# Spectral mixing and a two-layer MLP in split fp32: weight split earlier, high parts first, half of layer 0's casts on ScalarE

## The chip, the cores and the metric

The kernel runs on one core of one Trainium2 chip. What is compared is the device time of one execution in microseconds, the median of several runs. Within an execution, a trace of the hardware profiler tells when each instruction of each engine ran: TensorE (PE; its weight loads are PEld), VectorE (DVE), ScalarE (ACT), GpSimd (POOL), and SyncE (SP), which issues most of the transfers.

## What is computed

```python
X = np.fft.rfft(x, axis=1)                    # x: 2 x 3008 x 256
Yr = Xr @ w_r - Xi @ w_i + b_r
Yi = Xr @ w_i + Xi @ w_r + b_i
Y  = sign(Y) * max(|Y| - 0.01, 0)             # real and imaginary part, each
x  = np.fft.irfft(Y, n=3008, axis=1).reshape(6016, 256)
h  = x @ w_in1;  g = max(h, 0) + alpha * min(h, 0);        x = g @ w_out1     # 256 -> 2048 -> 256
h  = x @ w_in2;  g = h if h >= 1, 0 if h <= -1, else (h + 1)**2 / 4;  return g @ w_out2
```

The weights of the MLP layers are float64; everything is wanted with an accuracy beyond that of one reduced product, so each fp32 operand of the large products is split into a rounded high part and the rest, the low part, and a product is made of three: low x high, high x low, high x high.

## The kernel before, in words

**Stages.** The transform over 3008 = 47 x 64 points is done in two steps. First, `f1(g)` for 16 groups of inputs (8 for each of the 2 sequences): products with a 96 x 96 constant, copied out by ScalarE and VectorE in turn, stored to a scratch `a_dr` in DRAM (`store_a`) and loaded again in another order (`load_a`, in six parts for each sequence; `A_PARTS` gives first column and number of columns, and part (6, 6) holds the columns of items 3 to 5). Then 24 items (b, i) run through `f2` (second transform step), `mix` (product with the complex weights, soft threshold) and `i1` (first step of the inverse transform); item j's `mix` runs behind item j + 2's `f2`, apart from the first, where `f2` of items 2 and 3 follows `mix` of item 0. `p3` is the last step of the inverse transform. The two MLP layers follow.

**Mixing.** The weights `wm32[k]` are loaded by SyncE (lines 279 and 281), and `split` (lines 86 to 92) makes the high part as a cast on ScalarE (line 89) or VectorE (line 91) and the low part as a subtraction on VectorE (line 92). For the weights this is done behind the last `f1` (lines 302 to 304). An item's own parts are made in `f2`: high parts on ScalarE (lines 319, 320), low part on VectorE (line 321), its negated piece on ScalarE (line 322). `mix` has 24 products an item, in groups low x high, high x low, high x high (lines 335 to 337), the one with the item's low part first.

**MLP.** Each layer goes through 12 chunks of tokens (512 columns, chunks 5 and 11 have 448). For each chunk there are 16 steps f. `first(l, c, f)` makes six products into a PSUM bank (`psh`), then the nonlinearity: in layer 0 two relus on ScalarE into `ta` and `tb` (lines 447, 448) and a combination on VectorE (line 450), in layer 1 a relu on ScalarE and two operations on VectorE. The result is split into `gh` and `gl`. `ta` and `tb` have two buffers each, `gh` and `gl` four. `second(l, c, f)` makes six products of `gh` and `gl` into two banks that sum up over the 16 steps (`pso`); at f = 15 ScalarE copies the two banks out (line 479). The order is written out by hand in the last loop (lines 534 to 563): at each position `first` of one step, then side work, then `second` of the step three positions back (`DEPTH`). Each engine works through its own instructions in program order.

**Late and early casts.** `late_split` (line 421) names the steps whose cast is done late: all of layer 1, chunks 0, 1 and 11 of layer 0. There `split_late` inside the *next* step's `first` (line 449) issues the cast on ScalarE, behind that step's relus, and the subtraction on VectorE, ahead of that step's combination. For the other chunks of layer 0, 2 to 10, cast and subtraction follow the combination at once, both on VectorE (line 452).

**Side work in layer 0.** The weights of layer 1 are converted from float64 by a generator, `conversions`; each `next(conv)` (line 553) issues one piece, in chunks 2 to 10 on steps f = 0, 4, 8, 12. A piece in two parts: every second `next` issues a cast and two conversions on ScalarE (lines 175, 146, 147), two operations on VectorE (164, 148) and a multiplication and a clamp on GpSimd (165, 180); the one after that an operation on VectorE (159) and a subtraction and an addition on GpSimd (169, 170), which GpSimd can begin as soon as the first are done. On f = 8 `prep` splits the next chunk's input (128 x 1024: a cast on ScalarE, a subtraction on VectorE).

Of the kernel before, what the change touches and what calls it, by code (L numbers as in the profile page):

```python
# [9 lines left out]
F32R = mybir.dt.float32r  # L10
# [6 lines left out]
B, S, D = 2, 3008, 256  # L17
# [4 lines left out]
NF = DFF // 128  # L22
# [53 lines left out]
def spectral_mlp_kernel(ctx: ExitStack, tc: tile.TileContext, x, w_r, w_i, bias, c_f1, c_f2,  # L76
                        c_i1, c_i2, w_in1, w_out1, alpha, w_in2, w_out2, out):
    nc = tc.nc
    V, A, G, T = nc.vector, nc.scalar, nc.gpsimd, nc.tensor
# [6 lines left out]
    def split(src, hi, lo, hi_engine):  # L86

        if hi_engine is A:
            A.activation(hi, src, AF.Copy)  # L89
        else:  # L90
            V.tensor_copy(hi, src)  # L91
        V.tensor_tensor(lo, src, hi.bitcast(F32), op=ALU.subtract)  # L92
# [10 lines left out]
    def block(tag, shape, dtype, name):  # L103
        return base.tile(shape, dtype, tag=tag, name=name)
# [77 lines left out]
    def conversions(l, fs, clamp, low_engine):  # L182

        n = len(fs)
        for f in fs[:2]:
            load_w(l, f)
            yield
        for k in range(n + 1):
            if k >= 1:
                convert_w(l, fs[k - 1], 2, clamp, low_engine)  # L190
            if k < n:
                convert_w(l, fs[k], 0, clamp, low_engine)
            yield
            if k >= 1:
                convert_w(l, fs[k - 1], 3, clamp, low_engine)
            if k < n:
                convert_w(l, fs[k], 1, clamp, low_engine)
            if k + 2 < n:
                load_w(l, fs[k + 2])
            yield  # L200
# [23 lines left out]
    A_PARTS = ((0, 2), (2, 2), (4, 2), (6, 6), (12, 6), (18, 6))  # L224

    def load_a(b, parts):
        if a_sb[b] is None:
            a_sb[b] = block(f"a{b}", [128, NK, D], F32, f"a_{b}")
        for k, n in parts:
            h, k0 = divmod(k, NK // 2)  # L230
            src = a_dr[b][h].rearrange("t (q k) f -> (t q) k f", q=4)
            nc.sync.dma_start(a_sb[b][:, k:k + n, :], src[:, k0:k0 + n, :])
# [13 lines left out]
    def f1(g):  # L246
        b, j = divmod(g, 8)
        if g < 10:
            ae = block(f"w{8 + g}" if g < 5 else f"m{1 + g}" if g < 8 else f"w{g - 8}", [96, 4, D], F32, f"ae{g}")
        else:  # L250
            if g == 10:
                late.append(block("a1", [96, 6, 4, D], F32, "ae_late"))
            ae = late[0][:, g - 10]
        aes[g] = ae
        for i in range(2):
            ps = psum.tile([96, 2, D], F32, tag="h" if i else "o", name=f"ps1_{b}_{j}_{i}")
            for u in range(2):
                T.matmul(ps[:, u, :], c47, xs[g][:, 2 * i + u, :], start=True, stop=True)  # L258
            if i == 0:
                A.activation(ae[:, 0:2, :], ps, AF.Copy)  # L260
            else:
                V.tensor_copy(ae[:, 2:4, :], ps)
# [6 lines left out]
    wm32 = [rot.tile([128, 2, D], F32, tag="tb", name=f"wm32_{k}") for k in range(2)]  # L269
# [7 lines left out]
        if g == 3:  # L277
            load_mn(0, m_t, c_f2, 0)
    nc.sync.dma_start(wm32[0], w_r.rearrange("(c p) e -> p c e", p=128))
    load_a(0, A_PARTS[:1])  # L280
    nc.sync.dma_start(wm32[1], w_i.rearrange("(c p) e -> p c e", p=128))
    load_a(0, A_PARTS[1:2])
    nc.sync.dma_start(b_t[:, 0, :], bias)
    load_mn(0, m_t, c_f2, 1)
    load_a(0, A_PARTS[2:4])
# [8 lines left out]
    load_mn(2, m_t, c_f2)  # L294
    conv = conversions(0, list(range(NF)), V, V)
    next(conv)
    for g in range(8, 16):
        f1(g)
        store_a(g, 0)
    wm = [block(f"c{k}", [128, 2, 2, D], F32R, f"wm{k}") for k in range(2)]  # L300

    for k in range(2):
        hi, lo = (wm[k][:, z].rearrange("p c (h q) -> p c q h", h=2) for z in range(2))
        split(wm32[k].rearrange("p c (q h) -> p c q h", h=2), hi, lo, A)


    items = [(b, i) for b in range(B) for i in range(NK // 2)]
# [17 lines left out]
    def mix(b, i):  # L325
        xh, xl = xt.pop((b, i))
        ps = psum.tile([128, 2, D], F32, tag="o", name=f"psm{b}_{i}")
        for k in range(2):
            o = ps[:, k, :].rearrange("p (q h) -> p q h", h=2)
            for c in range(2):  # L330
                j = 2 * k + c
                for r, off in ((0, 64), (1, 0)):
                    last = c == 1 and r == 1
                    wh, wl = (wm[r][:, z, c, :].rearrange("p (h q) -> p q h", h=2) for z in range(2))
                    T.matmul(o, xl[:, j, off:off + 128], wh, start=c == r == 0, stop=False)  # L335
                    T.matmul(o, xh[:, j, off:off + 128], wl, start=False, stop=False)  # L336
                    T.matmul(o, xh[:, j, off:off + 128], wh, start=False, stop=last)  # L337
        cl_ = rot.tile([128, 2, D], F32, tag="ta", name=f"clip{b}_{i}")
        t = rot.tile([128, 2, D], F32, tag="tb", name=f"t{b}_{i}")
        y32 = rot.tile([128, 2, D], F32, tag="gh", bufs=4, name=f"y32_{b}_{i}")  # L340
        V.tensor_tensor(t, ps, b_t.to_broadcast([128, 2, D]), op=ALU.add)
        V.tensor_scalar(cl_, t, LAM, -LAM, op0=ALU.min, op1=ALU.max)
        V.tensor_tensor(y32, t, cl_, op=ALU.subtract)
        y_32[b, i] = y32
# [21 lines left out]
    NC = len(chunks)  # L366
# [52 lines left out]


    def late_split(step):
        return step[0] == 1 or step[1] < 2 or step[1] == NC - 1

    def split_late(step):
        if step is not None and late_split(step):
            split_g(step, A)
# [56 lines left out]
    n = len(items)  # L483
# [3 lines left out]
    for j in range(n):  # L487
# [23 lines left out]
        if j >= P3_AT:  # L511
            g = j - P3_AT
# [21 lines left out]
    for i in range(len(seq) + DEPTH):  # L534
        if i < len(seq):
            l, c, f = seq[i]
            if (l, c, f) == (0, 2, 0):
                for _ in conv:
                    pass
                conv = conversions(1, list(range(15)), G, G)  # L540
            if (l, c, f) == (0, NC - 1, 4):
                for _ in conv:
                    pass
                conv = conversions(1, [15], V, V)
            if i >= 1:
                first(l, c, f, seq[i - 1])
            if i == 2:
                prep(0, 1)
            if 8 <= i < 24 and i % 2 == 0:
                p3(4 + i // 2, 0)  # L550
                p3(4 + i // 2, 1)
            if 3 <= i < 2 * NF and i % 3 != 0 or l == 0 and c >= 2 and f % (2 if c == NC - 1 else 4) == 0:
                next(conv, None)
            if (l, c, f) == (0, 0, NF - 1):
                prep(0, 2)
            elif f == NF // 2 and (l, c) not in ((0, 0), (0, 1)):
                nxt = (l, c + 1) if c + 1 < NC else (l + 1, 0)
                if nxt[0] < 2:
                    prep(*nxt)
        elif i == len(seq):  # L560
            split_late(seq[-1])
        if i >= DEPTH:
            second(*seq[i - DEPTH])
# [30 lines left out]
```

## Time and profile before

| | us |
|---|---|
| median of 3 runs (lowest, highest) | 1153.89 (1153.33, 1154.28) |
| the profiled execution, device time | 1152.67 |
| span of its trace, first to last instruction | 1150.9 |
| TensorE busy | 1143.0 (99%) |
| VectorE busy | 905.9 (79%) |
| ScalarE busy | 633.4 (55%) |
| GpSimd busy | 85.1 (7%) |

The granted TensorE clock is 0.999 of full speed over the span. TensorE's busy time is modelled from pipelined products; how close it is to its limit is read from the distance of one product's start to the next. The chain that ended last is 93% TensorE and 4% VectorE.

### The profile page before, as it was taken

The numbers are of one execution on the slowest core, as the hardware profiler recorded it, in microseconds if no ns is written. First come the engines' busy times: TensorE is split into PE (matmuls) and PEld (weight loads), VectorE is DVE, ScalarE is ACT, GpSimd is POOL, SyncE is SP. The second block draws the span as 40 slices with busy tenths as digits, with TensorE's granted clock in tenths as the row PEclk, the third lists the DMA queues.
The fourth block names the chain that finished last, engine by engine and source line by source line (L and its number), as shares of the span: only waits on it lengthen the run. The fifth ranks groups of instructions, "written<-read, shape, count | busy, mean of one in ns | idle before, by whom it ended". The sixth has DMA issues, their size and how long they took to land.

```text
span 1150.9 us, 15833 instructions
## 1 busy us (share of the span) xinstructions
PE 1143.0 (99%) x5862; PEld 1026.1 (89%) x5862; DVE 905.9 (79%) x1409; ACT 633.4 (55%) x1131; POOL 85.1 (7%) x64
## 2 busy tenths in 40 slices
PE   9999999999999999999999999999999999999998
PEld 7899988988888988888889988888889988888898
DVE  3679977568899999999986687777777777777776
ACT  3455777675655655556555654545445454544544
POOL 0000000000132322312210000000000000000000
PEclk9999999999999999999999999999999999999999
DMA  9996561100010100100000000000000000000000
GB/s 290 311 306 206 187 189 41 56 1 1 19 37 20 37 19 19 37 19 19 1 1 19 1 1 19 1 19 19 19 1 19 17 1 19 19 19 1 20 19 16
DMA packets 37900, 59.30 MB, mean 52 GB/s; under 512 B 3328, under 2 KB 25280, under 8 KB 37824
## 3 DMA queue, kind: packets, MB, share of 16 engines
q1 hardware_dynamic: 37568, 58.15, 15.7%
q8 instruction: 46, 0.75, 0.3%
q14 instruction: 30, 0.25, 0.1%
q10 hardware_dynamic: 256, 0.15, 0.0%
HBM read 39.55 MB, written 18.74 MB: 51 GB/s over the span
## 4 chain that ended last, share of the span: by engine, by line
PE 93%; DVE 4%; ACT 1%; DMA 1%; issue 1%; SPq 0%; DVEq 0%; ACTq 0%
PE pso L96 13%; PE pso L97 13%; PE pso L95 13%; PE psh L95 13%; PE psh L97 13%; PE psh L96 13%; PE ps L258 2%; PE ps L416 2%; PE psm L335 2%; PE psm L337 2%; PE psm L336 2%; PE psi L350 2%; PE psf L314 2%; DVE gl L92 1%; DVE ta L450 1%; DVE gh L91 1%
## 5 line engine op out<-in xcount | busy, mean ns | idle before, releaser
L92 DVE TENSOR_TENSOR gl<-ta,gh 128x512 fp32r<-128x512 f32 (+1 forms) x384 | 273.5, 712 | 53.1 <-ACT gh L89 48.0
L96 PE MATMUL pso<-gl,w 128*128 128x512 f32 (+1 forms) x768 | 288.3, 375 | 1.2 <-DVE gl L92 1.1
L95 PE MATMUL pso<-gh,w 128*128 128x512 f32 (+1 forms) x768 | 288.4, 376 | 0.0
L95 PE MATMUL psh<-mxh,w 128*128 128x512 f32 (+1 forms) x768 | 288.2, 375 | 0.1
L96 PE MATMUL psh<-mxl,w 128*128 128x512 f32 (+1 forms) x768 | 287.8, 375 | 0.0
L97 PE MATMUL psh<-mxh,w 128*128 128x512 f32 (+1 forms) x768 | 287.7, 375 | 0.0
L97 PE MATMUL pso<-gh,w 128*128 128x512 f32 (+1 forms) x768 | 287.7, 375 | 0.0
L455 ACT ACTIVATE ta<-psh 128x512 f32<-128x512 f32 (+1 forms) x192 | 113.4, 591 | 242.9 <-PE psh L97 214.4
L447 ACT ACTIVATE ta<-psh 128x512 f32<-128x512 f32 (+1 forms) x192 | 113.3, 590 | 197.8 <-DVE gl L92 97.3
L456 DVE SCALAR_TENSOR_TENSOR tb<-ta 128x512 f32<-128x512 f32 (+1 forms) x192 | 130.8, 681 | 115.8 <-ACT ta L455 115.0
L450 DVE SCALAR_TENSOR_TENSOR ta<-ta,nalpha,tb 128x512 f32<-128x512 f32 (+1 forms) x192 | 157.8, 822 | 12.7 <-ACT tb L448 12.3
L96 PEld LDWEIGHTS pso<-gl,w 128*128 128x128 f32 x768 | 145.1, 189 | 20.3 <-DVE gl L92 3.1
L95 PEld LDWEIGHTS psh<-mxh,w 128*128 128x128 f32 x768 | 145.2, 189 | 17.8 <-ACT tb L448 0.5
L96 PEld LDWEIGHTS psh<-mxl,w 128*128 128x128 f32 x768 | 145.2, 189 | 17.6 <-DVE mxl L92 0.3
L97 PEld LDWEIGHTS psh<-mxh,w 128*128 128x128 f32 x768 | 145.2, 189 | 17.2
L95 PEld LDWEIGHTS pso<-gh,w 128*128 128x128 f32 x768 | 145.2, 189 | 17.1 <-DVE gh L91 0.2
L97 PEld LDWEIGHTS pso<-gh,w 128*128 128x128 f32 x768 | 145.2, 189 | 17.1
L89 ACT ACTIVATE gh<-ta 128x512 fp32r<-128x512 f32 (+1 forms) x240 | 147.4, 614 | 1.3 <-DVE ta L458 1.3
L458 DVE TENSOR_TENSOR ta<-psh,tb 128x512 f32<-128x512 f32 (+1 forms) x192 | 129.1, 672 | 0.0
L448 ACT ACTIVATE tb<-psh 128x512 f32<-128x512 f32 (+1 forms) x192 | 112.2, 584 | 0.0
L91 DVE CAST gh<-ta 128x512 fp32r<-128x512 f32 (+1 forms) x144 | 71.6, 497 | 15.2 <-DVE ta L450 0.5
L335 PE MATMUL psm<-wm,fl 128*128 128x256 f32 x192 | 54.9, 286 | 1.5 <-DVE fl L321 1.5
(56 smaller groups left out, 935.0 us busy)
## 6 DMA issues: line engine op xcount, KB each, us to landing
u<-in_w_in SPq DMA_DIRECT2D x32, 256.0 KB, 2.9
u<-in_w_out SPq DMA_DIRECT2D x32, 256.0 KB, 3.3
v_dr<-ve SPq DMA_DIRECT2D x12, 512.0 KB, 3.5
v<-v_dr SPq DMA_DIRECT2D x16, 384.0 KB, 5.6
x<-in_x SPq DMA_DIRECT2D x15, 384.0 KB, 7.6
out<-yt SPq DMA_DIRECT2D x20, 256.0 KB, 2.0
a<-a_dr SPq DMA_DIRECT2D x6, 768.0 KB, 7.3
a_dr<-ae SPq DMA_DIRECT2D x20, 192.0 KB, 6.7
```

The source lines that it names most:

```text
L89: A.activation(hi, src, AF.Copy)
L91: V.tensor_copy(hi, src)
L92: V.tensor_tensor(lo, src, hi.bitcast(F32), op=ALU.subtract)
L95: T.matmul(ps, wl, xh, start=start, stop=False)
L96: T.matmul(ps, wh, xl, start=False, stop=False)
L97: T.matmul(ps, wh, xh, start=False, stop=stop)
L447: A.activation(ta, ps, AF.Relu, scale=-1.0)
L448: A.activation(tb, ps, AF.Relu)
L450: V.scalar_tensor_tensor(ta, ta, nalpha[:, f:f + 1], tb, op0=ALU.mult, op1=ALU.add)
L455: A.activation(ta, ps, AF.Relu, bias=0.5, scale=0.5)
L456: V.scalar_tensor_tensor(tb, ta, 1.0, ta, op0=ALU.min, op1=ALU.mult)
L458: V.tensor_tensor(ta, ps, tb, op=ALU.max)
```

## The change

The weights of the mixing are split inside the loop of the last eight `f1`, the first behind group 13, the second behind group 14. The second weight is loaded ahead of the first part of the spectrum instead of behind it. `mix` takes, for each of the two weights, first the item's high part with the weight's low part, then high with high, then the item's low part. In layer 0, chunks 2 to 10, every second step (f odd) is cast late on ScalarE. The pieces of the conversion come on steps f = 2, 6, 10, 14 of these chunks.

```diff
     nc.sync.dma_start(wm32[0], w_r.rearrange("(c p) e -> p c e", p=128))
-    load_a(0, A_PARTS[:1])
     nc.sync.dma_start(wm32[1], w_i.rearrange("(c p) e -> p c e", p=128))
-    load_a(0, A_PARTS[1:2])
+    load_a(0, A_PARTS[:2])
...
+    wm = [block(f"c{k}", [128, 2, 2, D], F32R, f"wm{k}") for k in range(2)]
     for g in range(8, 16):
         f1(g)
         store_a(g, 0)
-    wm = [block(f"c{k}", [128, 2, 2, D], F32R, f"wm{k}") for k in range(2)]
-
-    for k in range(2):
-        hi, lo = (wm[k][:, z].rearrange("p c (h q) -> p c q h", h=2) for z in range(2))
-        split(wm32[k].rearrange("p c (q h) -> p c q h", h=2), hi, lo, A)
+        if g in (13, 14):
+
+            hi, lo = (wm[g - 13][:, z].rearrange("p c (h q) -> p c q h", h=2) for z in range(2))
+            split(wm32[g - 13].rearrange("p c (q h) -> p c q h", h=2), hi, lo, A)
...
-            for c in range(2):
-                j = 2 * k + c
-                for r, off in ((0, 64), (1, 0)):
-                    last = c == 1 and r == 1
-                    wh, wl = (wm[r][:, z, c, :].rearrange("p (h q) -> p q h", h=2) for z in range(2))
-                    T.matmul(o, xl[:, j, off:off + 128], wh, start=c == r == 0, stop=False)
-                    T.matmul(o, xh[:, j, off:off + 128], wl, start=False, stop=False)
-                    T.matmul(o, xh[:, j, off:off + 128], wh, start=False, stop=last)
+
+            for n, (r, x, z) in enumerate(((0, xh, 1), (0, xh, 0), (0, xl, 0), (1, xh, 1), (1, xh, 0), (1, xl, 0))):
+                for c in range(2):
+                    off = 0 if r else 64
+                    T.matmul(o, x[:, 2 * k + c, off:off + 128], wm[r][:, z, c, :].rearrange("p (h q) -> p q h", h=2),
+                             start=n == c == 0, stop=n == 5 and c == 1)
...
     def late_split(step):
-        return step[0] == 1 or step[1] < 2 or step[1] == NC - 1
+        return step[0] == 1 or step[1] < 2 or step[1] == NC - 1 or step[2] % 2 == 1
...
-            if 3 <= i < 2 * NF and i % 3 != 0 or l == 0 and c >= 2 and f % (2 if c == NC - 1 else 4) == 0:
+            if 3 <= i < 2 * NF and i % 3 != 0 or l == 0 and c >= 2 and (
+                    f % 2 == 0 if c == NC - 1 else f % 4 == 2):
                 next(conv, None)
```

## Rows read from the trace of the kernel before

**Rows 1.** The page, part 1: busy us, share of the span, instructions.
```profile
PE 1143.0 (99%) x5862; PEld 1026.1 (89%) x5862; DVE 905.9 (79%) x1409; ACT 633.4 (55%) x1131; POOL 85.1 (7%) x64
```

**Rows 2.** Table by stages: stretch, us, busy (instructions) PE, PEld, DVE, ACT, POOL; clock, DMA.
```profile
500.00:600.00 100.00, 100.00 (x465) 87.50 (x464) 92.60 (x131) 55.61 (x96) 26.98 (x19) 1.00 0.04 11
```

**Rows 3.** Timeline of TensorE, chunks 5 and 6: start, us, engine, line, operation.
```profile
402.41 0.42 PE L95 MATMUL pso<-gh,w 128*128 128x448 f32 x1
403.98 0.46 PE L96 MATMUL pso<-gl,w 128*128 128x448 f32 x1 [1.15 <-DVE gl L92]
...
443.74 0.38 PE L95 MATMUL pso<-gh,w 128*128 128x512 f32 x1
444.15 0.48 PE L96 MATMUL pso<-gl,w 128*128 128x512 f32 x1
```

**Rows 4.** Timeline of ScalarE, VectorE and TensorE, start of the mixing.
```profile
32.17 2.06 ACT L89 ACTIVATE wm<-wm 128x512 fp32r<-128x512 f32 x2
34.51 0.41 ACT L320 ACTIVATE fh<-psf 128x256 fp32r<-128x256 f32 x1
...
35.24 0.66 DVE L321 TENSOR_TENSOR fl<-psf,fh 128x512 fp32r<-128x512 f32 x1
...
35.95 0.38 PE L335 MATMUL psm<-wm,fl 128*128 128x256 f32 x1 [1.49 <-DVE fl L321]
38.85 2.00 PE L314 MATMUL psf<-m,a 128*128 128x128 f32 x16
```

**Rows 5.** Timeline of SyncE: parts (4, 2) and (6, 6) of the spectrum issued.
```profile
31.27 0.91 SPq L232 DMA_DIRECT2D a<-a_dr  x2
```

**Rows 6.** Transfers issued at 31.7 to 31.8 us: KB, us from issue to landing.
```profile
a<-a_dr SPq DMA_DIRECT2D x1, 768.0 KB, 7.8
```

**Rows 7.** Timeline of VectorE in chunk 3, casts early.
```profile
302.04 0.43 DVE L91 CAST gh<-ta 128x512 fp32r<-128x512 f32 x1
302.50 0.69 DVE L92 TENSOR_TENSOR gl<-ta,gh 128x512 fp32r<-128x512 f32 x1
303.11 0.75 DVE L450 SCALAR_TENSOR_TENSOR ta<-ta,nalpha,tb 128x512 f32<-128x512 f32 x1
303.96 0.43 DVE L91 CAST gh<-ta 128x512 fp32r<-128x512 f32 x1
```

**Rows 8.** Timeline of ScalarE and VectorE, end of chunk 1, casts late.
```profile
251.13 0.60 ACT L447 ACTIVATE ta<-psh 128x512 f32<-128x512 f32 x1 [0.82 <-DVE gl L92]
252.10 0.63 ACT L89 ACTIVATE gh<-ta 128x512 fp32r<-128x512 f32 x1
...
252.77 0.69 DVE L92 TENSOR_TENSOR gl<-ta,gh 128x512 fp32r<-128x512 f32 x1 [1.07 <-ACT gh L89]
...
253.55 0.60 ACT L447 ACTIVATE ta<-psh 128x512 f32<-128x512 f32 x1 [0.82 <-DVE gl L92]
```

**Rows 9.** Timeline of VectorE, GpSimd and ScalarE around a GpSimd burst, chunk 3.
```profile
296.36 1.45 DVE L450 SCALAR_TENSOR_TENSOR ta<-ta,nalpha,tb 128x512 f32<-128x512 f32 x1 [0.27 <-ACT tb L448]
297.92 0.65 DVE L91 CAST gh<-ta 128x512 fp32r<-128x512 f32 x1
298.60 1.65 DVE L92 TENSOR_TENSOR gl<-ta,gh 128x512 fp32r<-128x512 f32 x1
300.18 1.76 DVE L450 SCALAR_TENSOR_TENSOR ta<-ta,nalpha,tb 128x512 f32<-128x512 f32 x1
...
295.78 1.49 POOL L165 TENSOR_TENSOR cp<-cp,u 128x512 f32<-128x512 f32 x1 [21.76 <-DVE cp L164]
...
293.14 0.63 ACT L175 ACTIVATE w<-cm 128x512 fp32r<-128x512 f32 x1
...
295.28 0.57 ACT L447 ACTIVATE ta<-psh 128x512 f32<-128x512 f32 x1
...
298.32 2.04 ACT L479 ACTIVATE yt<-pso 128x512 f32<-128x512 f32 x2
```

**Rows 10.** Timeline of VectorE in chunk 5, 448 columns.
```profile
385.77 0.68 DVE L450 SCALAR_TENSOR_TENSOR ta<-ta,nalpha,tb 128x448 f32<-128x448 f32 x1
```

## The prediction

> **What bounds the kernel now.** I read the page's busy times first: TensorE is busy for 1143.0 of 1150.9 us [rows 1]. Next the table by stages: between 500 and 600 us TensorE has no idle time and issues 465 products, 0.215 us apart, while VectorE is busy for 92.6 us and ScalarE for 55.6 [rows 2]. TensorE's work isn't changed, so all that can be won is what TensorE waits; all that can be lost is a helper engine that falls behind it. Then TensorE's timeline, to find the few places where TensorE does wait. There are two that this change touches. In the first MLP layer, in the 448-column chunk 5, the product with the low part comes 1.57 us after the one before it instead of 0.19 (1.38 lost), and in chunk 6 0.41 instead of 0.215 (0.2); both wait for VectorE's subtraction L92 [rows 3]. With the slower issue of one product behind each, these are **1.7 us** together. At the start of the mixing TensorE waits 1.49 us for the low part of the first item [rows 4].
>
> **Edit 1: weight split between the transforms, high parts first.** It removes no instruction, and where the weights' blocks are reserved costs nothing. Today ScalarE's two casts (2.06 us) and VectorE's two subtractions stand just ahead of item 0's casts, which end at 34.51 + 0.41 = 34.92, and its subtraction, which ends at 35.90 [rows 4]. Made behind groups 13 and 14 they lie beside TensorE's transforms; item 0's casts are then between 0 and 2.06 us earlier; I take 0.5, as its own products are hardly done sooner, so its high part is there at about 34.4. With high parts first, TensorE starts on it then, and not at 35.95; the low part, needed four products later, comes about 0.15 too late for that. Mixing item 0 would end 35.95 - 34.4 - 0.15 = 1.4 us earlier than 38.85 [rows 4]. ScalarE may wait for the second weight, but that is asked for about 4 us earlier than now, while SyncE waits for stores anyway; its old issue, about 0.4 us, leaves the queue ahead of the spectrum loads.
>
> What is late next is the load of columns 6 to 11 of the spectrum. It is the second of the two issues that begin at 31.27 and last 0.91, so it begins at about 31.75 [rows 5], and lands 7.8 us later, at 39.55 [rows 6]. Transform item 3 needs it, and began eight products after 38.85, 16 taking 2.00, so at 39.75 to 39.85 [rows 4]: today the load already arrives just when it is used. The same bytes stand ahead of it as before, so it moves only by what SyncE and the transfer engines idle less. Bounds: not at all (gain 0) and as far as TensorE's own gain (1.4). I take **0.5 us**, one saved issue, the nearest row being those issues.
>
> The Trainium skill (page "DMA: Bandwidth & Descriptors", terms on queues, "HWDGE ordering") says that on each transfer engine descriptors are consumed in ring order. By that rule alone the bytes ahead of the load stay what they were, the gain is 0 and the whole sum below is +7.3 instead of +6.8; the trace's landing of 39.55 just ahead of its use agrees with it, and can't tell the half microsecond.
>
> **Edit 2: every second cast on ScalarE, in chunks 2 to 10 of layer 0.** 72 casts L91 of 0.43 us leave VectorE, 72 of 0.63 go to ScalarE. Nothing of the other work is removed. The point is the order: the ScalarE cast of an odd step is issued in the *next* step, behind that step's two relus, and VectorE's subtraction L92 of the odd step, for which it waits, stands ahead of everything that VectorE does for the even step. A relu may start only when the subtraction two steps back has freed its buffer (ta has two): at the end of chunk 1 the relus of late-cast steps waited 0.82 us for it [rows 8]. That closes a ring, and its length decides.
>
> Today, with early casts, a step costs VectorE 302.04 to 303.96 = **1.92 us**, cast to cast: cast to subtraction 0.46, to the next combination L450 0.61, to the next cast 0.85 [rows 7]; two steps are 3.84. New, for two steps, each piece from a row: relu to ScalarE cast 0.97, to L92 0.67, end of L92 (0.69) to the next relu 0.09 [rows 8]; in between 0.61, 0.85 and 0.46 as before [rows 7]. Sum: 0.97 + 0.67 + 0.61 + 0.85 + 0.46 + 0.69 + 0.09 = **4.34 us**. So VectorE does less, but the pair of steps gets longer, as VectorE now waits for ScalarE once in each. TensorE takes 24 x 0.215 = 5.2 us for a pair: alone, the ring keeps up.
>
> It doesn't run alone. A 512-column chunk is 16 x 12 x 0.215 = 41.3 us of TensorE. VectorE is busy for 0.926 x 41.3 = 38.2 of them [rows 2]; 16 x 1.92 = 30.7 are the steps, so 7.5 us are side work: the chunk's share of the weight conversion, the preparation of the next chunk, and the slowing by GpSimd. Most is the last: in one burst of four GpSimd instructions four VectorE operations took 1.45, 0.65, 1.65 and 1.76 instead of 0.75, 0.43, 0.69 and 0.75, that is 2.9 us more, and there are two bursts in a chunk [rows 9, 7]. Today 30.7 + 7.5 fit into 41.3 with 3 us to spare. New, the steps take 8 x 4.34 = 34.7. The bursts' 5.8 us come on top in full, since they stretch ring members themselves (L450 and L92 of the odd step, L450 of the even one). Of the other 1.7 us I let half hide in VectorE's new pauses: 0.9. And ScalarE is in the ring now: with the conversion on steps f = 2, 6, 10, 14 its 2.14 us (293.14 to 295.28) fall behind the same step f = 2 as the two copies of the finished chunk, 2.04 [rows 9]. Today they are two steps apart. I take 1.2 of these 4.2 us, the part that VectorE's burst doesn't cover. Sum: 34.7 + 5.8 + 0.9 + 1.2 = 42.6, **1.3 us more than TensorE's 41.3**. Bounds: all side work in the pauses (34.7, no wait at all), and none plus all 4.2 (46.4, 5 us a chunk).
>
> This is paid in chunks 4, 6, 7 and 8: 5.2. Chunk 3 starts with low parts ready some 2.8 us ahead of use and eats that up: 0.2. In chunk 9 GpSimd's burst comes in two pieces: 0.5. Chunk 5 has shorter products: 41.3 x 448 / 512 = 36.1, and with the two 512-column steps of its neighbour 36.6 of TensorE, while an operation as L450 shrinks only from 0.75 to 0.68 [rows 10, 7], the pair to about 4.0 (an estimate) and the chunk to 32 + 7.7 = 39.7: 3.1. Together 9.0, in which the old 1.7 are contained: **7.3 us more**. Moving the conversion steps does part the preparation from the burst, which is what made the old wait of 1.38; it is in the sums above as side work spread out.
>
> **Sum.** -0.5 + 7.3 = +6.8 us. The profiled execution took 1152.67 us, 1.8 around its span of 1150.9; the change would make it 1159.5. The median of the runs is 1.2 above it, at 1153.89, and with the same difference gives **1160.7 us**. A measurement of this kernel can tell about 0.2%, 2.3 us, from no change.
>
> **Rivals.**
> - *VectorE's load decides, not the ring (faster).* Then the lighter VectorE never lets TensorE wait: 1.7 + 0.5 = 2.2, with the mixing free of the load up to 3.1: 1150.8 to 1151.7. For it: VectorE at 92.6% [rows 2], and the waits come from there. Against it: the pieces of the ring are measured at the end of chunk 1, where every cast is late, and a step there takes 251.13 to 253.55 = 2.42 us, longer than 1.92 [rows 8, 7]. The Trainium skill says ("Perfetto Trace Analysis", "Optimizing Scalar/DVE Operations") that with VectorE saturated, offloading to ScalarE may make sense; that is this rival, and its time would be the one just given. The trace agrees that VectorE is nearly full, and speaks against the rest by the ring.
> - *The ring is longer, but the pauses take the side work in (no change).* The 512-column chunks then just fit, only chunk 5 waits, 1 to 3 us in place of 1.7: 1152.5 to 1155.
> - *The moved step doubles up worse.* If the 4.2 us of ScalarE at f = 2 come on top in full, a chunk costs 3 more than I took, six chunks 18: about 1179.
> - *The split does nothing* (load as late as before, gain 0): 1161.2, within the forecast.
>
> **How the numbers follow.** Forecast 0.60, its own range 1156.5 to 1165.5 (0.7 us a chunk either way over six chunks). Faster rival 0.15, four fifths of it over 2.3 us. No change 0.18. Much worse 0.07. Eight in ten: 1151.5 to 1165.5, which leaves out the worst case (0.07), the better part of the faster rival (0.08) and the forecast's tails (0.04). Faster by over 0.2%: 0.12. Within 0.2%: 0.20 (0.17 of the no-change case, 0.03 of the faster rival). Slower: 0.68 (0.60, 0.07 and 0.01 of the no-change case).
>
> **What would show it.** Right: TensorE idle on L92 in every chunk from 4 to 8, most in chunk 5, some 9 us in total; a 512-column chunk of 42 to 43 us; VectorE less busy than 92.6% there and waiting on ScalarE's L89. In the mixing: item 0 at about 34.4, then a new wait in front of item 3. Wrong: no waits of TensorE between 290 and 560 us although L89 stands in the chain, or VectorE's subtraction of odd steps well ahead of its use in all chunks.

## The result, and the profile after

The changed kernel takes **1160.62 us** (median of 6 runs, 1159.24 to 1161.06), the kernel before 1154.09 (6 runs, 1152.91 to 1155.37). The ratio is 1.0055, with a 95% interval of 1.0042 to 1.0068: slower, by 6.5 us. The forecast was 1160.7. Its profiled execution took 1160.89 us, with a span of 1159.1.

The page's first part, to be read against [rows 1]: VectorE is 46.5 us less busy, ScalarE 38.5 more, and TensorE, with the same 5862 products, 6.2 more.

```profile
PE 1149.2 (99%) x5862; PEld 1026.0 (89%) x5862; DVE 859.4 (74%) x1337; ACT 671.9 (58%) x1203; POOL 79.9 (7%) x64
```

The table by stages, the same 100 us as in [rows 2]: VectorE's 92.60 has become 78.24, and yet TensorE issues 456 products instead of 465. Nine products of 0.215 us are 1.9 us lost in this stretch.

```profile
500.00:600.00 100.00, 99.35 (x456) 85.49 (x456) 78.24 (x113) 67.86 (x118) 22.37 (x17) 1.00 0.03 11
```

The list of waits (engine, line, what it waited for: us in total, times, longest). VectorE's wait for the ScalarE cast L89 and TensorE's for VectorE's low part L92 lead to the same place: the late cast. Layer 1, where all casts were late before too, is in these totals.

```profile
DVE gl L92 <- ACT gh L89: 115.0, 110, 3.0
ACT ta L444 <- DVE gl L92: 101.3, 93, 2.8
PEld pso L96 <- DVE gl L92: 11.2, 23, 1.2
```

TensorE's timeline shows what comes out of it, in chunk 5 (448 columns) and chunk 7. In chunk 5 the first row waits for a high part, the two others for low parts. In chunk 7, one of the many small waits, the product comes 0.32 us after the one before it instead of 0.215, and the next one again 0.32.

```profile
392.30 0.46 PE L95 MATMUL pso<-gh,w 128*128 128x448 f32 x1 [0.96 <-ACT gh L89]
393.31 0.46 PE L96 MATMUL pso<-gl,w 128*128 128x448 f32 x1 [0.55 <-DVE gl L92]
...
412.59 0.46 PE L96 MATMUL pso<-gl,w 128*128 128x448 f32 x1 [0.86 <-DVE gl L92]
...
478.08 0.38 PE L95 MATMUL pso<-gh,w 128*128 128x512 f32 x1
478.40 0.48 PE L96 MATMUL pso<-gl,w 128*128 128x512 f32 x1
478.72 0.38 PE L97 MATMUL pso<-gh,w 128*128 128x512 f32 x1
```

**Where the time went, by stages.** A stage is measured here from the start of its first product to that of the next stage's (us, from the traces).

| stage | before | after | difference |
|---|---|---|---|
| start to the first product of `f2` | 32.34 | 34.81 | +2.47 |
| first product of `f2` to the first of the MLP (154.18; 155.16) | 121.84 | 120.35 | -1.49 |
| MLP to chunk 2 | 95.06 | 95.06 | 0.0 |
| chunks 2 to 10 of layer 0 | 369.63 | 377.13 | +7.50 |
| chunk 11 to the end of TensorE's work | 528.11 | 527.83 | -0.28 |

The first line is no work of the change. Between 2 and 10 us TensorE got through 19 products in this execution and 30 in that of the kernel before; two of the kernels below have 19 too, the others 26 to 32, among them kernels with each of the edits (last section). Without that line the sum is +5.7 us, with it +8.2; the medians say +6.5.

### The profile page after: what moved, and what is told of

It is laid out like the page before. It is cut to its first block, busy times and chain, and to the rows that moved or that the text cites. A ratio compares the mean times of both kernels' runs of the same rounds, so it can differ in the third digit from the quotient of the medians.

```text
span 1159.1 us, 15703 instructions
## 1 busy us (share of the span) xinstructions
PE 1149.2 (99%) x5862; PEld 1026.0 (89%) x5862; DVE 859.4 (74%) x1337; ACT 671.9 (58%) x1203; POOL 79.9 (7%) x64
## 3 DMA queue, kind: packets, MB, share of 16 engines
HBM read 39.55 MB, written 18.74 MB: 50 GB/s over the span
## 4 chain that ended last, share of the span: by engine, by line
PE 80%; DVE 11%; ACT 7%; issue 2%; DVEq 0%; ACTq 0%
PE pso L96 11%; PE pso L95 11%; PE pso L97 11%; PE psh L95 11%; PE psh L96 11%; PE psh L97 11%; PE psm L333 6%; DVE ta L447 5%; DVE gl L92 3%; PE ps L258 3%; PE ps L413 2%; ACT gh L89 2%; PE psi L347 2%; PE psf L313 2%; ACT ta L444 1%
## 5 line engine op out<-in xcount | busy, mean ns | idle before, releaser
L92 DVE TENSOR_TENSOR gl<-ta,gh 128x512 fp32r<-128x512 f32 (+1 forms) x384 | 267.4, 696 | 117.6 <-ACT gh L89 115.0
L89 ACT ACTIVATE gh<-ta 128x512 fp32r<-128x512 f32 (+1 forms) x312 | 192.6, 617 | 17.0 <-DVE ta L447 14.2
L447 DVE SCALAR_TENSOR_TENSOR ta<-ta,nalpha,tb 128x512 f32<-128x512 f32 (+1 forms) x192 | 164.0, 854 | 10.9 <-ACT tb L445 10.9
L333 PE MATMUL psm<-wm,fh 128*128 128x256 f32 x384 | 60.5, 280 | 0.0
L333 PEld LDWEIGHTS psm<-wm,fh 128*128 128x128 f32 x384 | 50.6, 192 | 0.0
```

Of the source, the lines that this page charges most:

```text
L333: T.matmul(o, x[:, 2 * k + c, off:off + 128], wm[r][:, z, c, :].rearrange("p (h q) -> p q h", h=2), start=n == c == 0, stop=n == 5 and c == 1)
L447: V.scalar_tensor_tensor(ta, ta, nalpha[:, f:f + 1], tb, op0=ALU.mult, op1=ALU.add)
```

## The experiments

The two theories at the start: **the ring** (a late cast makes a pair of steps 0.5 us longer, and with the side work that passes TensorE's time for a chunk), and **the load** (VectorE's and ScalarE's amounts of work decide; the order doesn't). Stage times are as in the table above: chunks 2 to 10 of layer 0 take 369.63 us in the kernel before and, as it will turn out, 367.8 without any wait of TensorE. Ratios are to the kernel before on the same chip, with their 95% intervals.

### One edit at a time

**The mixing alone**, with casts and conversion steps as before:

```diff
-        return step[0] == 1 or step[1] < 2 or step[1] == NC - 1 or step[2] % 2 == 1
+        return step[0] == 1 or step[1] < 2 or step[1] == NC - 1
...
-                    f % 2 == 0 if c == NC - 1 else f % 4 == 2):
+                    f % (2 if c == NC - 1 else 4) == 0):
```

> Edit 1 alone: weights split between the transforms, high parts first; casts and conversion as in the kernel before. My theory: -0.5 us, between 0 and -1.5, because the load of spectrum columns 6 to 11 lands at about 39.0 us and TensorE, ready some 0.9 us earlier, waits for it ahead of transform item 3. Rival (the mixing's start is what counts, no load behind it): -1.4 us. The two waits of chunks 5 and 6 on L92 (1.7 us) stay, in both.

1152.47 us against 1153.48, ratio 0.9989 (0.998 to 0.9998). Chunks 2 to 10 take 369.63, exactly as before; the time from the last `f1` product to the MLP is 0.99 us shorter. Its trace shows a wait of 0.27 us in front of `f2` for a load of the spectrum, which takes part of the gain. The medians, 1.0 us apart, can't tell my theory (0.5) from the rival (1.4); the trace shows no wait in front of item 3, where my theory wanted one.

**The late casts alone**, on the kernel before:

```diff
-        return step[0] == 1 or step[1] < 2 or step[1] == NC - 1
+        return step[0] == 1 or step[1] < 2 or step[1] == NC - 1 or step[2] % 2 == 1
```

> Of edit 2 the late casts alone, conversion still on f = 0, 4, 8, 12. Ring theory (a pair of steps takes 4.34 us of ScalarE and VectorE in turn, plus the GpSimd bursts): slower by 4 to 9 us, TensorE waiting on L92 in every chunk from 3 or 4 to 8; the copies of the finished chunk (f = 2) and the conversion (f = 0) no longer fall together, some 1 us a chunk less, but the preparation falls into a burst again, some 1 us a chunk more. Rival (the moved conversion steps do the harm, not the cast's place): within 1 us of the kernel before, or faster.

1161.92 us, ratio 1.007 (1.0058 to 1.0083). Chunks 2 to 10 take 378.82: 9.2 us more, as the ring theory had it. The late casts make the whole loss, and more of it without the other edits.

**The conversion steps alone**, on the kernel before:

```diff
-            ... f % (2 if c == NC - 1 else 4) == 0:
+            ... (f % 2 == 0 if c == NC - 1 else f % 4 == 2):
```

> Of edit 2 the conversion steps alone (f = 2, 6, 10, 14), all casts of chunks 2 to 10 early on VectorE. Ring theory: the preparation and the GpSimd burst no longer meet, the waits of chunks 5 and 6 go: -1.0 to -1.7 us. Rival (the moved steps do the harm): slower by several us, new waits of TensorE in chunks 4 to 8.

1154.30 us, ratio 1.0005 (0.9997 to 1.0014). Chunks 2 to 10 take 369.96. Neither theory had that. The old waits don't go away, they move: chunk 5 still waits, now 0.39 us behind the product at 389.6, 0.49 behind that at 408.2 and 0.40 behind that at 411.1.

**Mixing and conversion steps, without the late casts** (the first of the diffs above, applied to the changed kernel):

> Edit 1 and the moved conversion steps, no late casts in chunks 2 to 10. Ring theory: the sum of both parts, -1.5 to -2.7 us against the kernel before, 8 to 9 us faster than the changed kernel. Rival (moved steps do the harm): as slow as the changed kernel, +5 to +7.

1152.98 us, ratio 0.9994 (0.9985 to 1.0003); chunks 2 to 10 take 369.94, the way from the first `f2` to the MLP 120.35, as in the changed kernel. I had expected 1.5 to 2.7 us less, and 0.5 less was measured: the conversion steps give back nothing. In the stages of these traces the edits add up: -1.5 for the mixing, +0.3 for the conversion steps alone, and the late casts on top.

### The cast ahead of the relus

Here an odd step's cast and subtraction are issued ahead of the next step's relus. Each engine has the same instructions as in the changed kernel; their order is different.

```diff
+            ahead = before is not None and 2 <= before[1] < NC - 1
+            if ahead:
+                split_late(before)
             A.activation(ta, ps, AF.Relu, scale=-1.0)
             A.activation(tb, ps, AF.Relu)
-            split_late(before)
+            if not ahead:
+                split_late(before)
```

> The changed kernel, with one difference in chunks 3 to 9 of layer 0: the late cast and subtraction of an odd step are issued ahead of the next step's two relus instead of behind them. Every engine has the same instructions; only their order differs. Ring theory: the two relus (0.57 + 0.40 us) no longer stand between the odd step's combination and its cast, so the ring of two steps falls from 4.34 us to some 4.0, a chunk of 512 columns from 42.6 to 40.1, which is below TensorE's 41.3: only chunk 5 (37.3 against 36.6) still waits, 0.7 us. Chunk 2 to chunk 11 then takes 370 to 371 us instead of 377.1, and the kernel 1153 to 1155. Rival (the loss comes of ScalarE's greater load or of the total of the moved work, not of the order): as the changed kernel, 377 us and 1160.6.

1169.23 us, ratio 1.0133 (1.012 to 1.0147); chunks 2 to 10 take 385.5. A miss: slower than the changed kernel by 8.4 us in these chunks, where I expected it some 6 faster. With the same work on each engine the time moved by 8 us, so the load theory falls as well; order it is. My ring for it was wrong. ScalarE's and VectorE's timelines (start, us) show why:

```profile
466.00 0.75 DVE L450 SCALAR_TENSOR_TENSOR ta<-ta,nalpha,tb 128x512 f32<-128x512 f32 x1
...
466.78 0.63 ACT L89 ACTIVATE gh<-ta 128x512 fp32r<-128x512 f32 x1 [2.37 <-DVE ta L450]
...
467.32 0.58 ACT L446 ACTIVATE ta<-psh 128x512 f32<-128x512 f32 x1
...
467.80 0.59 ACT L447 ACTIVATE tb<-psh 128x512 f32<-128x512 f32 x1
...
468.42 0.75 DVE L450 SCALAR_TENSOR_TENSOR ta<-ta,nalpha,tb 128x512 f32<-128x512 f32 x1 [0.28 <-ACT tb L447]
...
470.35 0.75 DVE L450 SCALAR_TENSOR_TENSOR ta<-ta,nalpha,tb 128x512 f32<-128x512 f32 x1
```

The relus no longer stand between combination and cast, but now the cast stands in front of the next relus: from the odd step's combination (466.00) to the cast 0.78, to the relus 0.54 and 0.48, to the even step's combination 0.62, to the next odd one 1.93. Together 4.35 us for the pair, no shorter than before. And more of the side work shows. Counted from the ends of the 16 subtractions of chunk 7, as for the changed kernel in the next section, eight pairs are 34.8 us, and 9.2 come on top where the changed kernel has 7.9: VectorE's share of the conversion costs 0.6 twice (0.23 there), the preparation 1.1 (0.8), the burst beside the copies 3.6 (3.3). A chunk takes 44.0 us.

### A third buffer for the relus' output

```diff
...
-        gl = rot.tile([128, NMAX], F32R, tag="gl", bufs=4, ...)
-        ta = rot.tile([128, NMAX], F32, tag="ta", ...)[:, :n]
+        gl = rot.tile([128, NMAX], F32R, tag="gl", bufs=3, ...)
+        ta = rot.tile([128, NMAX], F32, tag="ta", bufs=3, ...)[:, :n]
```

> The changed kernel with three buffers for the relus' output ta instead of two (and three instead of four for the low part gl, to make room). The order of work is the same. Ring theory: the ring is closed by the relu that waits until the subtraction two steps back has freed ta; with a third buffer that wait falls away, and a chunk is bound by VectorE's and ScalarE's own work again, some 40 us for 512 columns: chunk 2 to chunk 11 370 to 372 us, the kernel 1153 to 1156. Rival (order on VectorE alone decides: the subtraction of the odd step waits for ScalarE at the head of VectorE's queue, whatever the buffers): 376 to 378 us, the kernel about 1160.6. Second rival (three buffers for gl are too few, as VectorE's subtraction must then wait for TensorE's products): above 1160.6.

1156.16 us, ratio 1.0022 (1.0014 to 1.0031); chunks 2 to 10 take 374.1, where I expected 370 to 372. Of the 7.5 us lost there, 3.0 come back. VectorE's timeline for a pair of steps:

```profile
457.38 0.69 DVE L92 TENSOR_TENSOR gl<-ta,gh 128x512 fp32r<-128x512 f32 x1
...
460.04 0.69 DVE L92 TENSOR_TENSOR gl<-ta,gh 128x512 fp32r<-128x512 f32 x1 [0.69 <-ACT gh L89]
...
462.03 0.69 DVE L92 TENSOR_TENSOR gl<-ta,gh 128x512 fp32r<-128x512 f32 x1
...
464.08 0.69 DVE L92 TENSOR_TENSOR gl<-ta,gh 128x512 fp32r<-128x512 f32 x1 [0.69 <-ACT gh L89]
...
466.07 0.69 DVE L92 TENSOR_TENSOR gl<-ta,gh 128x512 fp32r<-128x512 f32 x1
```

From 462.03 to 466.07 are 4.04 us: the wait for `ta` is gone, but VectorE still stands idle once in each pair, 0.69 us, for ScalarE's cast, and 4.04 is more than the 3.84 of two early steps. 457.38 to 462.03 holds 0.6 us of conversion besides. Eight pairs of chunk 7 are 32.3 us; the side work on top, counted as before, is 9.8, more than the changed kernel's 7.9. Together that is the 42.1 us that the chunk takes, still over TensorE's 41.4. So the buffers are two fifths of the loss. What is left is the hand-over itself, and side work that the shorter pauses don't take in.

### Without GpSimd's bursts

```diff
-                clamp_w(l, f, G)
+                pass
...
-            E.tensor_tensor(p, p, low, op=ALU.mult)
+            if E is not G:
+                E.tensor_tensor(p, p, low, op=ALU.mult)
...
-            E.tensor_tensor(m, m, wt[l, f][:, 0, :].bitcast(F32), op=ALU.subtract)
-            E.tensor_tensor(wt[l, f][:, 1, :], m, p, op=ALU.add)
+            if E is G:
+                G.memset(wt[l, f][:, 1, :].bitcast(F32), 0.0)
+            else:
+                ...
```

> The changed kernel without GpSimd's arithmetic on the weights of the second MLP layer: the clamp and the low part of those weights are left out (the low part is written as zero), so the output of layer 1 is a rougher one. TensorE's work is unchanged. Ring theory: the 5.8 us a chunk by which GpSimd's bursts stretch VectorE's operations go, a chunk of 512 columns is 34.7 + about 2 = 37 us against TensorE's 41.3, and chunk 5 34 against 36.6: no waits in chunks 3 to 9, chunk 2 to chunk 11 367.5 to 368.5 us, the kernel 1150.5 to 1152. Rival (the ring alone makes the wait, the bursts hide in its pauses): as the changed kernel, 377 us, 1160.6.

1150.60 us, ratio 0.9968 (0.9956 to 0.998); chunks 2 to 10 take 367.84. The table by stages for most of a chunk has 192 products in 41.0 us, no idle time on TensorE, and VectorE at 28.96:

```profile
460.00:501.00 41.00, 41.00 (x192) 35.90 (x191) 28.96 (x47) 27.68 (x49) 0.00 (x0) 1.00 0.08 26
```

All 72 casts are late here, and TensorE waits for nothing in chunks 2 to 10. The late casts lose time only together with the bursts.

### Every fourth cast

```diff
-        return ... or step[1] == NC - 1 or step[2] % 2 == 1
+        return ... or step[1] == NC - 1 or step[2] % 4 == 1
```

> The changed kernel with every fourth cast of chunks 2 to 10 on ScalarE instead of every second: 36 casts moved instead of 72. Ring theory: four steps take 4.34 + 3.84 us, a chunk of 512 columns 32.7 + 7.9 = 40.6, below TensorE's 41.3, and chunk 5 about 37.7 against 36.6: the waits are 1 to 2 us in all, chunk 2 to chunk 11 369.5 to 371 us, the kernel 1152.5 to 1154. Rival (each late cast costs its own wait, whatever the sum over a chunk): half the loss, 373 to 374 us, the kernel 1156 to 1157.

1163.00 us against 1153.13, ratio 1.0074 (1.0061 to 1.0086); chunks 2 to 10 take 379.1, 9.5 more than before. (The mixing gains 1.5 of that back; the profiled execution had the longer start of the table above.) Half the casts moved, and the loss isn't smaller. Both theories missed. The timeline of VectorE, GpSimd and TensorE at step 3 of chunk 7 (the changed kernel's rows of the same step are in the next section):

```profile
474.23 0.75 DVE L447 SCALAR_TENSOR_TENSOR ta<-ta,nalpha,tb 128x512 f32<-128x512 f32 x1 [1.56 <-ACT tb L445]
...
474.38 1.74 POOL L169 TENSOR_TENSOR cm<-cm,w 128x512 f32<-128x512 f32 x1
...
475.08 1.31 DVE L91 CAST gh<-ta 128x512 fp32r<-128x512 f32 x1
...
476.19 1.33 POOL L170 TENSOR_TENSOR w<-cm,cp 128x512 fp32r<-128x512 f32 x1
...
476.43 1.64 DVE L92 TENSOR_TENSOR gl<-ta,gh 128x512 fp32r<-128x512 f32 x1
...
478.12 0.48 PE L96 MATMUL pso<-gl,w 128*128 128x512 f32 x1 [1.18 <-DVE gl L92]
```

The burst falls on step 3, whose cast is early here: cast and subtraction, both on VectorE, take 1.31 and 1.64 us instead of 0.43 and 0.69. From the end of step 2's low part to that of step 4's are 8.10 us, 4.26 more than two early steps. In the changed kernel step 3 is late, its cast is on ScalarE, VectorE waits anyway, and the same two steps take 7.68, only 3.34 more than their 4.34. So side work isn't a fixed sum on top of the ring: **it costs less in a step that has a pause**, and the 0.5 us of a late cast are lost where there is nothing to put in its pause. This third theory can be tried with the same number of casts.

### The same number of casts, in other steps

Late casts in steps 3, 7, 11, 15, where the bursts fall:

```diff
-        ... or step[2] % 2 == 1
+        ... or step[2] % 4 == 3
```

> The changed kernel with a late ScalarE cast in steps f = 3, 7, 11, 15 of chunks 2 to 10, instead of in every odd step. It has as many late casts (36) as the kernel with f = 1, 5, 9, 13, which lost 9.9 us. Theory of this run (a late cast makes its step 0.5 us longer, but only where VectorE has nothing else to do in the pause; the burst of GpSimd, the conversion and the copies fall on the low parts of steps 3 and 4 and of 11 and 12): with the late cast in those very steps the two steps take 7.68 us as in the changed kernel instead of 8.11, so the lead of the low parts is better by 0.4 us at each burst than with all casts early, and the steps 7 and 15 cost 0.13 each, as VectorE's part of the conversion fills their pause. Chunk 2 to chunk 11: 368.5 to 369.7 us, the kernel 1151.3 to 1152.8. Rival (the number of late casts decides): as with f = 1, 5, 9, 13, 379 us and 1161 to 1163.

1151.36 us, ratio 0.9985 (0.9976 to 0.9994); chunks 2 to 10 take 368.98. As many late casts as in the run before, and 11.6 us faster.

Late casts in steps 3 and 11 alone (`step[2] % 8 == 3`):

> The changed kernel with a late ScalarE cast in steps f = 3 and 11 of chunks 2 to 10 alone, 18 casts. Theory: as with f = 3, 7, 11, 15, without the 0.13 us of steps 7 and 15: chunk 2 to chunk 11 368.3 to 369.5 us, the kernel 1151 to 1152.5. Rival (each late cast costs the same, a quarter of the 9 us of 72 or half of the 9 us of 36): 372 to 374 us, the kernel 1155 to 1157.

1151.82 us, ratio 0.9978 (0.9969 to 0.9987); chunks 2 to 10 take 368.44.

The steps 1, 5, 9, 13 again, which lost 9.9 us, but with the conversion, and so the bursts, back on the old steps, so that these fall on steps 1 and 9:

```diff
-        ... or step[2] % 2 == 1
+        ... or step[2] % 4 == 1
...
-                    f % 2 == 0 if c == NC - 1 else f % 4 == 2):
+                    f % 2 == 0 if c == NC - 1 else f % 4 == 0):
```

> The changed kernel with a late ScalarE cast in steps f = 1, 5, 9, 13 (the 36 casts that lost 9.9 us), and the weight conversion on its old steps f = 0, 4, 8, 12. Theory: now the bursts fall on the low parts of steps 1 and 2 and of 9 and 10, where late casts stand; the two steps take 7.67 us instead of 7.89 and 8.78 instead of 9.02, against 0.14 us for each of steps 5 and 13: chunk 2 to chunk 11 369 to 370 us, as in the kernel before (369.6), and the kernel, with the gain of the mixing, 1151.8 to 1153.2. Rival (the number of late casts decides, wherever the conversion stands): 377 to 379 us, 1160 to 1163. Second rival (the conversion's old steps are themselves worse with late casts, as they were with every second one, 1.7 us): 379 us or more.

1151.14 us, ratio **0.9974** (0.9965 to 0.9983), the lowest median of the kernels here that compute everything, though the intervals don't part it from the two before it; chunks 2 to 10 take 368.22, a little less than I expected, with one wait of TensorE left that the trace shows, 0.28 us in chunk 5. Two kernels with the same 36 late casts in the same steps, with 379.1 and 368.2 us for chunks 2 to 10: where the late casts stand against the bursts decides, not how many there are.

## Why the prediction came out right, point by point

**The ring.** It held to the hundredth. ScalarE's and VectorE's timelines of the changed kernel, chunk 7, steps 0 to 2:

```profile
465.63 0.69 DVE L92 TENSOR_TENSOR gl<-ta,gh 128x512 fp32r<-128x512 f32 x1
...
466.42 0.60 ACT L444 ACTIVATE ta<-psh 128x512 f32<-128x512 f32 x1 [0.83 <-PE pso L96]
...
467.39 0.63 ACT L89 ACTIVATE gh<-ta 128x512 fp32r<-128x512 f32 x1
...
468.05 0.69 DVE L92 TENSOR_TENSOR gl<-ta,gh 128x512 fp32r<-128x512 f32 x1 [1.06 <-ACT gh L89]
...
468.66 0.74 DVE L447 SCALAR_TENSOR_TENSOR ta<-ta,nalpha,tb 128x512 f32<-128x512 f32 x1
...
469.51 0.43 DVE L91 CAST gh<-ta 128x512 fp32r<-128x512 f32 x1
...
469.97 0.69 DVE L92 TENSOR_TENSOR gl<-ta,gh 128x512 fp32r<-128x512 f32 x1
```

The subtraction's end to the relu 0.10, the relu to the ScalarE cast 0.97, to L92 0.66, then 0.61, 0.85, 0.46; with the 0.69 of the first subtraction itself, from 465.63 to 469.97 the pair takes 4.34 us, put together from [rows 7, 8] of a stage with other casts. (The relu's wait is put down to a product of TensorE; it starts 0.10 behind the end of the subtraction that frees `ta`, and in the later steps the same wait is put down to L92.)

**The side work and the chunk.** The burst at step 3, on VectorE the odd step's subtraction, the even step's combination, stretched to 1.76 us, and the even step's subtraction:

```profile
473.09 1.76 POOL L169 TENSOR_TENSOR cm<-cm,w 128x512 f32<-128x512 f32 x1
...
474.45 0.95 DVE L92 TENSOR_TENSOR gl<-ta,gh 128x512 fp32r<-128x512 f32 x1 [0.74 <-ACT gh L89]
...
474.93 1.61 POOL L170 TENSOR_TENSOR w<-cm,cp 128x512 fp32r<-128x512 f32 x1
...
475.32 1.76 DVE L447 SCALAR_TENSOR_TENSOR ta<-ta,nalpha,tb 128x512 f32<-128x512 f32 x1
...
477.65 0.69 DVE L92 TENSOR_TENSOR gl<-ta,gh 128x512 fp32r<-128x512 f32 x1
```

Counted from the ends of the 16 subtractions of chunk 7: eight pairs of 4.34 are 34.7; 3.34 more at steps 3 and 4, 3.35 at 11 and 12, where the second burst falls; 0.77 at step 9 (the next chunk's preparation) and twice 0.23 (VectorE's share of the conversion). That is 42.6 us from chunk to chunk, the forecast's 42.6, against 41.4 without waits. The relus start 1.1 to 3.9 us behind the end of their products in every step, so TensorE doesn't set the pace. Chunks 7 and 8 took 42.63 and 42.61, chunks 4 and 6 42.46 and 42.24. TensorE's waits with the slower issue behind them are 377.1 - 367.8 = 9.3 us, where 9.0 was forecast; the MLP became 7.2 us longer, where 7.3 was.

That the sums fit so well is in part luck, as terms inside them were off and made up for each other. Chunk 5 was put at 39.7 and took 40.75: it lost 3.95 us, counted from the kernel without bursts, where 3.1 was forecast, and the other chunks lost 5.3, where 5.9 was. Inside a chunk the bursts were put at 5.8 and cost 6.7, the small work at 0.9 and cost 1.2, and the doubling at f = 2 at 1.2 and cost nothing (below). And there never were "3 us to spare" in the kernel before: that came of VectorE's busy time, which leaves out what it waits for during the bursts. With all casts early the side work costs 10.6 us a chunk (4.3 and 4.0 for the bursts, 1.1 for the preparation, twice 0.6 for the conversion, counted in the same way in the kernel with the conversion steps alone), and 30.7 + 10.6 = 41.3 is just TensorE's time. The 7.9 that I added in the new kernel came out right for it, but not for my reason, half of the small work in the pauses: the pauses take 2.7 of the 10.6. The kernel with every fourth cast shows what that is worth: four late steps more, 2.0, with 10.5 of the 10.6 still on top, 43.2 us; its chunks 4 and 6 to 8 took 42.5 to 43.25.

Beside the bursts VectorE's operations are stretched: 1.76 us instead of 0.74 for this combination. The Trainium skill ("SBUF — State Buffer", "Who interferes with whom") says that a VectorE instruction with two inputs in SBUF contends with a GpSimd instruction that reads SBUF, and that the one that comes second is fully blocked. The rows fit that roughly: the combination ends at 477.08, 0.54 us behind the recorded end of GpSimd's L170 (476.54), where it takes 0.74 by itself; GpSimd's ends are rough.

**The doubling at f = 2.** Of ScalarE's 4.2 us, 1.2 were taken to come on top. In the changed kernel the copies of the finished chunk fall beside the first burst of chunk 7 (ScalarE's timeline):

```profile
469.98 2.04 ACT L476 ACTIVATE yt<-pso 128x512 f32<-128x512 f32 x2
```

The second burst has no copies beside it, and yet the two cost the same, 3.34 and 3.35. The doubling isn't free by itself: without the bursts, steps 3 and 4 take 6.39 us instead of 4.34, as ScalarE's relu comes 2.9 us behind its product there. Beside the burst it just doesn't add up with it. With the conversion on the old steps, and late casts in every odd step, chunks 2 to 10 are 1.7 us longer (378.8), not shorter: that rival is out.

**The mixing: the term that was mis-sized.** -0.5 was forecast, between 0 and -1.4; it was -1.5. TensorE's timeline at its start:

```profile
34.81 1.95 PE L313 MATMUL psf<-m,a 128*128 128x128 f32 x16
36.55 0.71 PE L333 MATMUL psm<-wm,fh 128*128 128x256 f32 x4
37.55 0.49 PE L333 MATMUL psm<-wm,fl 128*128 128x256 f32 x2 [0.29 <-DVE fl L320]
...
39.89 1.28 PE L313 MATMUL psf<-m,a 128*128 128x128 f32 x10
```

SyncE's timeline, with the two loads of the spectrum of which the second, issued at 31.67, was to be late next:

```profile
24.68 0.39 SPq L280 DMA_DIRECT2D wm<-in_w_i  x1
...
31.19 0.91 SPq L232 DMA_DIRECT2D a<-a_dr  x2
```

And its row among the transfers issued at 31.6 to 31.8 us (KB, us from issue to landing):

```profile
a<-a_dr SPq DMA_DIRECT2D x1, 768.0 KB, 7.0
```

Item 0's own part went as forecast: high parts first, and a wait for the low part inside it. From the first `f2` product to `f2` of item 2 it is 5.08 us, where it was 38.85 - 32.34 = 6.51 [rows 4]: 1.43 gained, the whole of TensorE's own gain. The step that failed is the load as next bound. It landed at 31.67 + 7.0 = 38.7 us, and the products of item 3 began at 40.78, without a wait; none of the 13 traces has a wait there.

Why the load wasn't late is only in part known. `f1` ended 2.5 us later in this execution, which by itself leaves the load more time. In the kernel with mixing and conversion steps, which has no such late start, it landed at 30.82 + 7.1 = 37.9, with item 3 beginning at 38.45. The weight's 256 KB, which stood between the spectrum's loads, now go out at 24.68 instead of at 28.30, and I had counted the bytes and not when the transfer engines get them. But that this brought the load forward is not shown: it landed at 38.5 also in the two kernels without this edit (the late casts alone, the conversion steps alone), and at 37.0 to 39.4 in the ten with it. The 39.55 that I took as fixed was the value of one execution. The sentence of the Trainium skill beside that term ("DMA: Bandwidth & Descriptors", "HWDGE ordering") is not contradicted by any of these traces, but the gain of 0 that I worked out from it, with the landing held at 39.55, is.

The 1.5 us aren't a fixed gain either. Counted from the last `f1` product to the MLP, five of the ten kernels with the edit are 1.5 us shorter than the kernel before; with the mixing alone it is 1.0. In three more (the third buffer, late casts in steps 3 and 11, and in 1, 5, 9, 13 with the old conversion steps) it is 0.75 to 0.85, as TensorE waits 0.74 us for item 0's low part instead of 0.29. Without the bursts it is 0.3, with 0.92 us of waiting for the first load of the spectrum.

**The conversion steps.** The remark that moving them parts preparation and burst, and so removes the old wait of 1.38 us, was wrong: done alone, it left 2.1 us of waits in chunks 2 to 10, where there were 1.8. The wait moved with the bursts: in chunk 5 it is now at step 3, where the burst falls beside the copies of the finished chunk, and more of it at steps 11 and 12, where the other burst falls and no copies are.

**The sum.** -0.5 + 7.3 = 6.8 was forecast, -1.5 + 7.2 = 5.7 is what the stages show, and 6.5 is what the medians show. The difference of 0.8 between the last two is within the interval of the ratio (4.8 to 7.8 us); starts like the one of the profiled execution (last section) may have a part in it, which was not tried. The forecast's 1160.7 is so close to 1160.62 partly by luck.

## What to carry to other kernels

Moving work to a less busy engine doesn't shorten a chain in which both engines take turns: add up the ring of the hand-overs, through the buffers too, and compare that with the bound engine's time, side work included. Busy time is a poor measure of what is to spare, as an engine that is stretched by another also waits; count from end to end of the last operation. And place such a hand-over in the steps in which the receiving engine is held up anyway: there it was worth up to 1.4 us in these kernels, and a step or two beside it cost 9.5.

## What the runs showed of the hardware that I had not expected

- **The start differs between executions.** Between 2 and 10 us TensorE issued very different numbers of products (the first bracket of a row of the table by stages). In the kernel with mixing and conversion steps, and without the late casts:

```profile
2.00:10.00 8.00, 7.60 (x29) 5.23 (x29) 1.37 (x2) 2.25 (x4) 0.00 (x0) 1.00 1.02 263
```

In the changed kernel:

```profile
2.00:10.00 8.00, 8.00 (x19) 5.20 (x19) 0.69 (x1) 1.62 (x3) 0.00 (x0) 1.00 1.01 271
```

In the changed kernel behind that:

```profile
10.00:20.00 10.00, 10.00 (x47) 7.54 (x46) 3.97 (x6) 3.00 (x6) 0.00 (x0) 1.00 1.04 318
```

  The difference is TensorE's clock. In the changed kernel's trace its products start 0.43 us apart up to 10.4 us and 0.215 apart from there on, at half pace and then at full pace; in the kernel before the pace doubles at 5.6 us. The trace's record of the granted clock begins only then, at 10.35 and at 5.52 us, with 1.00, so the 1.00 of the first two rows says nothing of the time before; the half pace is that of the lower of the clock's two levels, 1.2 instead of 2.4 GHz. 4.8 us longer at half pace are 2.4 us of work, which is nearly the whole +2.47 of the first `f2`. In both executions TensorE had worked almost without a pause from 1.19 us on. The cast-ahead kernel and that with every fourth cast had 19 as well, the ten others of the study 26 to 32. Why the clock rises later in some executions stays open.
- **A wait costs more than its length.** In nearly every wait of TensorE for a low or high part that the traces show, the next product comes 0.10 us late as well, as in the last rows of TensorE's timeline above (0.32 instead of 0.215; with 448 columns, behind 393.31, 0.29 instead of 0.19).
- **Nothing is lost by late casts as such.** With the bursts gone, all 72 of them cost no wait at all, though the low parts were at most 3.5 us ahead of their use in chunk 7, where they were up to 4.7 ahead in the kernel before.
